# Queries loaded without their zero halves, a block's columns 18 elements apart, the zeros written once on the chip

## The chip, the cores and the metric

The kernel runs on one core of a Trainium2 chip. The metric is the device time of one execution in microseconds; 577.83 us is the median of three runs of the kernel before (577.48 to 578.81). A core has five engines that work side by side, each through its own list of instructions: PE (TensorE, matrix products), DVE (VectorE), ACT (ScalarE), POOL (GpSimd) and SP (SyncE, which here only issues DMA transfers). PE works through pairs of a weight load, which puts one operand into the array, and a matmul, which streams the other operand past it; the profile shows the weight loads as a row of their own, PEld.

## The reference

Two stages run one behind the other, for a batch of 8 sequences of 576 positions and 8 heads of 64. The first is attention with two masks (a window of 32 positions for heads 0 to 3, every fourth position of the last 128 for heads 4 to 7); the second is a mixer that multiplies by cosine and sine of a learned angle, mixes over positions with two matrices, and ends in a channel product with a ReLU.

```python
scores = scale * np.matmul(q, k.transpose(0, 1, 3, 2))
scores = np.where(masks[None, :, :, :], scores, -1000000000.0)
scores = scores - np.max(scores, axis=-1, keepdims=True)
attn = np.exp(scores)
attn = attn / (np.sum(attn, axis=-1, keepdims=True) + 1e-09)
x = np.matmul(attn, v)          # then heads side by side: (8, 576, 512)
theta = x @ w_theta
y = einsum('ts,bsd->btd', w_tok_r, x * cos(theta)) + einsum('ts,bsd->btd', w_tok_i, x * sin(theta))
u = x + y
out = u + np.maximum(u @ w_ch, 0.0)
```

## The kernel before

**Heads in pairs, blocks of 32.** The host reorders the positions of heads 4 to 7 so that both masks become the same band: a block of 32 queries (QB) meets 64 keys (BW). Heads are taken in pairs (NP = 4 pairs for each of the 8 sequences, so 32 pairs in all). A pair stands on 128 partitions, 64 for the depth of each head. One matmul gives the scores of a block for both heads: its weights are 128 x 64, 32 columns for the first head and 32 for the second, and the columns of one head are zero on the 64 partitions of the other. The kernel before gets these zeros from memory: `qT[b, pr]` is 128 x 18 x 64, half of it zeros, 576 KB a pair, and a block's 64 columns lie side by side in it (`q[:, qb]`, L468). The streamed operand is 64 columns of the keys, `k[:, QB*qb : QB*qb + BW]`. The 18 blocks of a pair alternate between the two halves of the output's partitions (`ps[64*e : 64*e+64]`, e = 0 and 1). In fp32 each such product is two weight loads and two matmuls in the profile, so a pair counts 36 of each.

**What follows the scores.** For sequence 0 and four pairs more, the masks are added by PE (L424) and the exponential reads the scores out of PSUM; for the others DVE adds the mask and takes the row maximum (L409) and ACT takes the exponential with its row sum (L504). POOL divides by the sum (L510), DVE turns the blocks (L525), PE multiplies by the values (L617), ACT copies the result out as `x` (L581; for pairs 2 and 3 it writes each element 4 elements, 16 bytes, behind the last, to put the positions back in their order). Then come the angle products (L667 for sequence 0, L685 to L692 for the others), cosine and sine on ACT (L796, L705), their products with `x` on DVE, a split of these into a high and a low part (ACT L644, POOL L646), the token products (L850) and the channel products (L882).

**Weights.** They come as 64-bit integers and are turned into numbers on the chip by `unpack` (DVE L332 and L342, ACT L334 and L340), which reads every second 32-bit word, and split by `split` (ACT L350, POOL L352): first `wth`, then the token weights `wtk`, last the channel weights `wch`.

**What sets the order.** PE's list is pinned everywhere to the order in which the program writes it. For sequence 0, and for the attention of sequence 1 and the start of sequence 2 beside it, a planner (`Order`) sets the order on all engines: each task names an engine and a cost, a DMA's cost is its bytes at a fixed rate (`dma(n)`), and tasks start by rank and by the events that they wait for. So a different cost of a load moves other work. From sequence 1's mixer on (`phase`), the order of PE is written out by tables, and the other engines' order follows from a scheduler.

**The queries' buffers.** `load_qk` takes one of two rotating slots (`take("qk", 2)`), gets a tile `q` of 128 x 18 x 64 from a pool with two buffers, and issues one DMA for q and one for k on SP's queue; after a pair's scores the slot is given back and the load of the pair two further on is issued. `first_loads` does the same for sequence 0 with q in the tiles that later hold `u`. A DMA issue on SP's queue also waits until the transfer eight issues earlier has landed, as the order of instructions shows by the semaphores named there.

Of the kernel before, what the change touches and what calls it, by code (L numbers as in the profile page):

```python
# [8 lines left out]
F32 = mybir.dt.float32  # L9
# [8 lines left out]
B, H, S, D = 8, 8, 576, 64  # L18
DM = H * D
NP = H // 2  # L20
QB = 32
BW = 2 * QB
NJ = S // (2 * QB)
# [38 lines left out]
class Order:  # L62
# [13 lines left out]
    def pin(self, ins):  # L76
        if self.live:
            self.tc.keep_in_program_order(ins)

    def signal(self, event):  # L80
        self.events[event] = self.now
# [49 lines left out]
def dve(n):  # L131
    return 67 + 1.04 * n
# [6 lines left out]
def act(n):  # L139
    return 95 + 0.83 * n  # L140
# [6 lines left out]
def dma(n):  # L147
    return 128 * 4 * n / 360.0
# [3 lines left out]
def build(ctx, tc, qT, kT, vw, wth, wtk, wch, maskb, ident, identb, outT):  # L152
    nc = tc.nc
    cp = ctx.enter_context(tc.tile_pool(name="const", bufs=1))
    ap = ctx.enter_context(tc.tile_pool(name="attn", bufs=2))
# [12 lines left out]
    pin, go, signal = od.pin, od.go, od.signal  # L168

    def pe(ins):  # L170
        tc.keep_in_program_order(ins)
# [27 lines left out]
    def give(tag, n):  # L199
        if od.live:  # L200
            signal(("free", tag, n))
# [11 lines left out]
    def load_qk(n):  # L213
        if n >= B * NP:
            return
        b, pr = divmod(n, NP)
        r = yield from take("qk", 2)
        q = ap.tile([128, 2 * NJ, 2 * QB], F32, tag="q", name=f"q{b}_{pr}")
        k = ap.tile([128, S + 32], F32, tag="k", name=f"k{b}_{pr}")
        yield "DMA", dma(2 * S)  # L220
        pin(nc.sync.dma_start(q, qT[b, pr]))
        yield "DMA", dma(S + 32)
        pin(nc.sync.dma_start(k, kT[b, pr]))
        qks[b, pr] = (q, k, r)
        signal(("qk", b, pr))
# [12 lines left out]
    def load_vb(n):  # L238
# [12 lines left out]
        vs["b", b, pr] = (vb, r)  # L251
        signal(("vb", b, pr))

    KE = S + 32
    first_k = hp.tile([128, 10 * HS], F32R, tag="wt_b", name="first_k").bitcast(F32)
    first_v = hp.tile([128, 8 * HS], F32R, tag="wt_a", name="first_v").bitcast(F32)
# [13 lines left out]
    def first_loads():  # L270
        yield "DMA", dma(3 * BW + 64)
        pin(nc.sync.dma_start(mskb, maskb.bitcast(BF16)))
        pin(nc.sync.dma_start(idb, identb.bitcast(BF16)))
        for pr in range(NP):
            yield from take(f"xh{pr}", 1, 0)
            yield from take(f"u{pr}", 1, 0)
            pqs.append(hp.tile([128, 2, S], F32R, tag=f"xh{pr}", name=f"P0_{pr}").bitcast(F32)[:, 0])
            q = hp.tile([128, 2, S], F32R, tag=f"u{pr}", name=f"q0_{pr}").bitcast(F32)
            q = q.rearrange("p a b -> p (a b)").rearrange("p (a b) -> p a b", b=2 * QB)
            k = first_k[:, KE * pr:KE * pr + KE]  # L280
            yield "DMA", dma(2 * S)
            pin(nc.sync.dma_start(q, qT[0, pr]))
            yield "DMA", dma(KE)
            pin(nc.sync.dma_start(k, kT[0, pr]))
            qks[0, pr] = (q, k, None)
            if pr == 0:
                yield "DMA", dma(128)
                pin(nc.sync.dma_start(idt, ident))
            signal(("qk", 0, pr))
        for pr in range(NP // 2):  # L290
            v = first_v[:, NJ * 128 * pr:NJ * 128 * pr + NJ * 128].rearrange("p (a b) -> p a b", b=128)
            yield "DMA", dma(NJ * 128)
            pin(nc.sync.dma_start(v, vw[0, pr]))
            for h, t in (("a", v[:, :VA]), ("b", v[:, VA:])):
                vs[h, 0, pr] = (t, None)
                signal(("v" + h, 0, pr))
        for pr in range(NP // 2, NP):
            yield from load_va(pr)
            yield from load_vb(pr)

    def consts():
        yield "DVE", 60
        pin(nc.vector.memset(halfpi, math.pi / 2))
        for n in range(2):
            t = cp.tile([128, NJ, 2, 2 * QB], F32, name=f"pt{n}")
            yield "POOL", 1040
            pin(nc.gpsimd.memset(t, 0.0))
            pts.append(t)
        signal("pts")

    def unpack(src, sz, name, stage, early, n, key):

# [102 lines left out]
    def on_pe(b, pr):  # L415
        return b == 0 or (b, pr) in ((1, 2), (1, 3), (2, 0), (2, 1))
# [24 lines left out]
    def scores(b, pr):  # L441
        yield None, ("qk", b, pr)
        if b == 1 and on_pe(b, pr):
            yield None, "sin0"
        if pr >= 1:
            yield None, ("sc", b, pr - 1)
        q, k, rqk = qks[b, pr]
        if b == 0:
            P, rp = pqs[pr].rearrange("p (a b) -> p a b", b=BW), None
        else:  # L450
            rp = yield from take("P", 2)
            P = sp.tile([128, NJ, BW], F32, tag="P", name=f"P{b}_{pr}")
        mx = sp.tile([128, NJ], F32, tag=f"mx{b == 0 and pr}", name=f"mx{b}_{pr}", bufs=1 if b == 0 else 2)
        sm = sp.tile([128, NJ], F32, tag=f"sm{b == 0 and pr}", name=f"sm{b}_{pr}", bufs=1 if b == 0 else 2)
        held = {}
        for g0, g1 in ((0, 5), (5, NJ)):
            ps, rel = yield from bank("s", f"s{b}_{pr}_{g0}")
            ps = ps[:, :(g1 - g0) * BW].rearrange("p (a b) -> p a b", b=BW)
            held[g0] = ps, rel
            masked = on_pe(b, pr)  # L460
            if masked:
                yield "PE", 150
                mask_on_pe(ps, pr, g0, g1)
            yield "PE", 162 * (g1 - g0)
            for n in range(g0, g1):
                for e in range(2):
                    qb = 2 * n + e
                    pe(nc.tensor.matmul(ps[64 * e:64 * e + 64, n - g0], q[:, qb],  # L468
                                        k[:, QB * qb:QB * qb + BW], start=not masked, stop=not masked or n == g1 - 1))
            if masked:  # L470
                go(row_max(b, ps, rel, P, mx, g0, g1, ("mask", b, pr, g0)))
            else:
                go(mask_scores(ps, rel, P, mx, pr, g0, g1, ("mask", b, pr, g0)))
        signal(("sc", b, pr))
        if b == 0:
            give(f"u{pr}", 0)
        else:
            give("qk", rqk)
            go(load_qk(b * NP + pr + 2), RANK["load"])
        if b and on_pe(b, pr):  # L480
            for g0, (ps, rel) in held.items():
                yield None, ("mask", b, pr, g0)
                yield "ACT", 335 * ps.shape[1]
                for n in range(ps.shape[1]):
                    table(nc.scalar.activation(P[:, g0 + n], ps[:, n], AF.Exp, bias=mx[:, g0 + n:g0 + n + 1],
                                               scale=SCALE, accum_out=sm[:, g0 + n:g0 + n + 1]))
                give(*rel)
        else:
            for g0 in (0, 5):
                yield None, ("mask", b, pr, g0)  # L490
        if b == 0:
            yield "ACT", act(S)
            table(nc.scalar.activation(P, P, AF.Exp, scale=SCALE))
            yield "DVE", dve(S)
            pin(nc.vector.tensor_reduce(sm, P, op=ALU.add, axis=mybir.AxisListType.X))
        elif not on_pe(b, pr):
            yield "DVE", 67
            pin(nc.vector.tensor_scalar(mx, mx, -SCALE, None, op0=ALU.mult))  # L498
            if b == 1:
                yield None, "sin0"  # L500
            for n0 in range(0, NJ, 3):
                yield "ACT", 720
                for n in range(n0, n0 + 3):
                    table(nc.scalar.activation(P[:, n], P[:, n], AF.Exp, bias=mx[:, n:n + 1], scale=SCALE,  # L504
                                               accum_out=sm[:, n:n + 1]))
        yield "DVE", 200
        pin(nc.vector.tensor_scalar(sm, sm, 1e-9, None, op0=ALU.add))
        pin(nc.vector.reciprocal(sm, sm))  # L508
        yield "POOL", 1110
        pin(nc.gpsimd.tensor_tensor(P, P, sm.unsqueeze(2).to_broadcast([128, NJ, BW]), op=ALU.mult))  # L510
        probs[b, pr] = P, rp
        signal(("P", b, pr))
# [482 lines left out]
def _arrays(inp):  # L995
    import numpy as np
    q, k, v = inp["q"], inp["k"], inp["v"]
# [5 lines left out]
        return a  # L1003

    q, k, v = perm(q), perm(k), perm(v)
    qT = np.zeros((B, NP, 2, D, 2 * NJ, 2, QB), q.dtype)
    qh = q.reshape(B, NP, 2, 2 * NJ, QB, D).transpose(0, 1, 2, 5, 3, 4)
    for hh in range(2):
        qT[:, :, hh, :, :, hh] = qh[:, :, hh]
    qT = qT.reshape(B, NP, 128, 2 * NJ, 2 * QB)  # L1010
    kT = np.zeros((B, NP, 128, S + 32), k.dtype)
    kT[..., 32:] = k.transpose(0, 1, 3, 2).reshape(B, NP, 128, S)
    vp = np.zeros((B, H, S + 32, D), v.dtype)
# [11 lines left out]
    for n, (j, bound) in enumerate(((1, 0), (0, 0), (2, 144), (4, 288), (6, 432), (7, 432))):  # L1025
        for quad in range(4):
            qb = 2 * j + quad // 2
            p = QB * qb + np.arange(QB)[:, None]
# [30 lines left out]
```

## Time and profile before

| | |
|---|---|
| median of three runs | 577.83 us |
| the profiled execution | 577.82 us |
| its span, first to last instruction | 576.0 us |
| mean granted PE clock | 0.988 |
| queries loaded | 32 DMAs of 576 KB, of 81.02 MB moved on SP's queue |
| score matmuls (L468) | 1152 records, 46.4 us busy |
| ACT busy, POOL busy | 345.2 us, 222.2 us |

Busy time is the sum of the records of an engine; on PE the records of neighbouring matmuls overlap, so what one costs in a run of them is the distance of their starts. In a row of a timeline stand the start, the time taken by the merged run, engine, line, operation, tiles, sizes, the number of instructions (x), and in brackets what the engine waited for. In a table by stretches stand, for each stretch, its length, and for each engine the busy time and in parentheses the number of instructions; then the granted PE clock, the busy share of the DMA engines and GB/s.

### The profile page before, as it was taken

The page shows a single profiled execution, that of the slowest core. Times are in us where ns is not written, and L with a number is a line of the kernel's source. Part 1 is how long each engine was busy: PE and PEld are TensorE (multiplying, and loading weights), DVE is VectorE, ACT ScalarE, POOL GpSimd, SP SyncE. Part 2 cuts the span into 40 slices and gives each one's busy share as a digit, 9 for nine tenths or more (in the row PEclk, how much of TensorE's full clock was granted, in tenths as well). Part 3 has the DMA queues.
Part 4 walks back from the last instruction along what each step waited for, and adds up shares of the span by engine and source line. Part 5 has one row for each costly group of instructions (what it writes and reads, how often), then busy time and mean ns, then how long its engine had stood idle before and what let it go on. Part 6 is the DMA issues. An engine that isn't in the chain of part 4 may idle for free.

```text
span 576.0 us, 13996 instructions
## 1 busy us (share of the span) xinstructions
PE 550.5 (96%) x5464; PEld 501.6 (87%) x5464; DVE 378.0 (66%) x1156; ACT 345.2 (60%) x939; POOL 222.2 (39%) x206
## 2 busy tenths in 40 slices
PE   5997799999999999999999999999999999999997
PEld 4744688879999899988999899988999899989997
DVE  3879798865666668756776768756775767445112
ACT  1498967768555784369555785359556695266110
POOL 2228855525224352226324253226323353325220
PEclk9999699899999999999999999999999999999999
DMA  8991437601747046540746146550747123321002
GB/s 303 400 368 28 165 105 245 216 0 63 231 150 193 32 162 210 169 127 20 268 143 172 64 148 202 181 136 11 252 146 190 69 83 102 77 89 65 18 1 83
DMA packets 45586, 81.91 MB, mean 142 GB/s; under 512 B 3920, under 2 KB 19024, under 8 KB 45520
## 3 DMA queue, kind: packets, MB, share of 16 engines
q1 hardware_dynamic: 45520, 81.02, 43.7%
q8 instruction: 43, 0.70, 0.5%
q14 instruction: 23, 0.19, 0.1%
HBM read 64.49 MB, written 16.52 MB: 141 GB/s over the span
## 4 chain that ended last, share of the span: by engine, by line
DVE 34%; ACT 30%; PE 25%; issue 5%; POOL 2%; DMA 2%; SPq 0%; ACTq 0%; POOLq 0%; DVEq 0%
DVE pt L525 16%; PE y L850 11%; ACT P L504 11%; PE c L882 6%; PE th L685 3%; DVE P L409 3%; ACT K L698 3%; ACT K L787 3%; DVE xh L599 3%; ACT th L796 2%; ACT zh L644 2%; DVE xq L729 2%; DVE K L789 2%; ACT cos L705 2%; ACT x L581 2%
## 5 line engine op out<-in xcount | busy, mean ns | idle before, releaser
L830 POOL TENSOR_TENSOR u<-x,u 128x288 fp32r<-128x288 f32 x64 | 54.7, 858 | 184.6 <-ACT u L828 184.6
L525 DVE STREAM_TRANSPOSE pt<-P 32x288 f32<-32x288 f32 x224 | 105.1, 469 | 12.0 <-POOL P L510 8.9
L882 PE MATMUL c<-u,late_wc 128*128 128x288 f32 x768 | 110.2, 296 | 2.8 <-DVE x L859 2.8
L882 PEld LDWEIGHTS c<-u,late_wc 128*128 128x128 f32 x768 | 106.0, 188 | 6.8 <-DVE x L859 4.0
L850 PE MATMUL y<-wtkh,zh 128*128 128x288 f32 x288 | 90.3, 314 | 1.1 <-ACT zh L644 1.1
L850 PE MATMUL y<-wtkh,zl 128*128 128x288 f32 x288 | 86.2, 299 | 4.0 <-POOL zl L646 4.0
L646 POOL TENSOR_TENSOR zl<-g,zh 128x512 fp32r<-128x512 f32 x40 | 52.3, 1316 | 97.5 <-ACT zh L644 84.5
L504 ACT ACTIVATE P<-P,mx 128x64 f32<-128x64 f32 x216 | 72.0, 335 | 25.8 <-DVE mx L498 25.8
L850 PE MATMUL y<-wtkl,zh 128*128 128x288 f32 x288 | 85.9, 298 | 0.0
L828 ACT CAST u<-x 128x288 fp32r<-128x288 f32 x64 | 26.9, 429 | 86.2 <-DVE x L825 85.5
L685 PE MATMUL th<-wthh,xh 128*128 128x512 f32 x224 | 74.8, 395 | 0.3 <-DVE g L784 0.3
L850 PE MATMUL y<-late_wt_b,zh 128*128 128x288 f32 x320 | 68.1, 297 | 0.0
L825 DVE TENSOR_TENSOR x<-y,x 128x288 f32<-128x288 f32 x64 | 28.1, 448 | 53.6 <-PE y L850 53.5
L850 PEld LDWEIGHTS y<-wtkh,zl 128*128 128x128 f32 x288 | 55.1, 191 | 4.7 <-POOL zl L646 4.7
L850 PEld LDWEIGHTS y<-wtkh,zh 128*128 128x128 f32 x288 | 54.9, 191 | 4.7 <-ACT zh L644 2.3
L850 PE MATMUL y<-late_wt_a,zh 128*128 128x288 f32 x256 | 56.3, 301 | 0.0
L850 PEld LDWEIGHTS y<-wtkl,zh 128*128 128x128 f32 x288 | 55.1, 191 | 0.3 <-issue 0.3
L510 POOL TENSOR_TENSOR P<-P,sm 128x576 f32<-128x576 f32 x32 | 37.5, 1172 | 41.1 <-DVE sm L508 18.1
L850 PEld LDWEIGHTS y<-late_wt_b,zh 128*128 128x128 f32 x320 | 51.4, 189 | 0.3
L685 PEld LDWEIGHTS th<-wthh,xh 128*128 128x128 f32 x224 | 42.0, 188 | 9.2 <-DVE g L784 0.6
L850 PE MATMUL y<-late_wt_b,zl 128*128 128x288 f32 x160 | 47.4, 296 | 0.0
L581 ACT COPY x<-o 128x576 f32<-128x576 f32 x32 | 29.4, 919 | 28.4 <-PE o L617 19.1
(108 smaller groups left out, 1106.3 us busy)
## 6 DMA issues: line engine op xcount, KB each, us to landing
q<-in_qT_dram SPq DMA_DIRECT2D x32, 576.0 KB, 5.2
va<-in_vw_dram SPq DMA_DIRECT2D x30, 320.0 KB, 3.2
k<-in_kT_dram SPq DMA_DIRECT2D x28, 304.0 KB, 5.5
out_dram<-x SPq DMA_DIRECT2D x28, 288.0 KB, 2.4
vb<-in_vw_dram SPq DMA_DIRECT2D x29, 256.0 KB, 3.8
xd<-xq SPq DMA_DIRECT2D x24, 288.0 KB, 5.1
xn<-xd SPq DMA_DIRECT2D x24, 256.0 KB, 3.4
st_wtk<-in_wtk_dram SPq DMA_DIRECT2D x8, 576.0 KB, 8.8
```

The source lines that it names most:

```text
L409: pin(nc.vector.tensor_tensor_reduce(out=P[:, n], in0=ps[:, n - g0], in1=mskb[:, mask_of(pr, n)], op0=ALU.add, op1=ALU.max, scale=1.0, sca ...
L504: table(nc.scalar.activation(P[:, n], P[:, n], AF.Exp, bias=mx[:, n:n + 1], scale=SCALE, accum_out=sm[:, n:n + 1]))
L510: pin(nc.gpsimd.tensor_tensor(P, P, sm.unsqueeze(2).to_broadcast([128, NJ, BW]), op=ALU.mult))
L525: pin(nc.vector.transpose(pmats[b, pr][k0:k0 + QB, :, hh, QB * e:QB * e + QB], P[p0:p0 + QB, :, QB * o:QB * o + QB]))
L581: pin(nc.scalar.copy(dst, src))
L646: pin(nc.gpsimd.tensor_tensor(lo, z, hi.bitcast(F32), op=ALU.subtract))
L685: pe(nc.tensor.matmul(pt, l, r, start=(n == 0), stop=(n == 3 * NC - 1)))
L825: pin(nc.vector.tensor_tensor(x[:, ts], ps, x[:, ts], op=ALU.add))
L828: pin(nc.scalar.copy(uh[b, d][:, ts], x[:, ts]))
L830: pin(nc.gpsimd.tensor_tensor(ul[b, d][:, ts], x[:, ts], uh[b, d][:, ts].bitcast(F32), op=ALU.subtract))
L850: pe(nc.tensor.matmul(ps, l[:, cs], r, start=(n == 0), stop=(n == 3 * NK - 1)))
L882: pe(nc.tensor.matmul(ps, l[:, cs], r[:, ts], start=(n == 0), stop=(n == 3 * NC - 1)))
```

## The change

The host no longer writes zeros: `qT` is 128 x 576 for a pair, with the element of position r of block n at column 18 r + n. On the chip q is 128 x 2 x 576, one half for each head; each head's 64 partitions are loaded into their own half by a DMA of their own, and the other half holds zeros. For the pairs of `load_qk` there are two fixed buffers `qbufs`, whose zeros POOL writes once at the start; for sequence 0's four pairs DVE writes the zeros into the four tiles. A block's weights are now `q[:, :, qb]` of a view whose 64 columns stand 18 elements (72 bytes) apart, through both halves.

```diff
 load_qk:
-        q = ap.tile([128, 2 * NJ, 2 * QB], F32, tag="q", name=f"q{b}_{pr}")
+        q = qbufs[r % 2]
         k = ap.tile([128, S + 32], F32, tag="k", name=f"k{b}_{pr}")
-        yield "DMA", dma(2 * S)
-        pin(nc.sync.dma_start(q, qT[b, pr]))
+        yield "DMA", dma(S)
+        for hh in range(2):
+            rs = slice(64 * hh, 64 * hh + 64)
+            pin(nc.sync.dma_start(q[rs, hh], qT[b, pr, rs]))
...
+    qbufs = [cp.tile([128, 2, S], F32, name=f"q{n}") for n in range(2)]
 first_loads:
             q = hp.tile([128, 2, S], F32R, tag=f"u{pr}", name=f"q0_{pr}").bitcast(F32)
-            q = q.rearrange("p a b -> p (a b)").rearrange("p (a b) -> p a b", b=2 * QB)
+            for hh in range(2):
+                pin(nc.vector.memset(q[64 * hh:64 * hh + 64, 1 - hh], 0.0))
...
-            yield "DMA", dma(2 * S)
-            pin(nc.sync.dma_start(q, qT[0, pr]))
+            yield "DMA", dma(S)
+            for hh in range(2):
+                rs = slice(64 * hh, 64 * hh + 64)
+                pin(nc.sync.dma_start(q[rs, hh], qT[0, pr, rs]))
 consts, behind the two memsets of pt:
+        for q in qbufs:
+            for hh in range(2):
+                yield "POOL", 580
+                pin(nc.gpsimd.memset(q[64 * hh:64 * hh + 64, 1 - hh], 0.0))
 scores:
+        q = q.rearrange("p h (r n) -> p (h r) n", n=2 * NJ)
...
-                    pe(nc.tensor.matmul(ps[64 * e:64 * e + 64, n - g0], q[:, qb],
+                    pe(nc.tensor.matmul(ps[64 * e:64 * e + 64, n - g0], q[:, :, qb],
                                         k[:, QB * qb:QB * qb + BW], start=not masked, stop=not masked or n == g1 - 1))
 _arrays:
-    qT = np.zeros((B, NP, 2, D, 2 * NJ, 2, QB), q.dtype)
...
+    qT = q.reshape(B, H, 2 * NJ, QB, D).transpose(0, 1, 4, 3, 2).reshape(B, NP, 128, S)
```

Line numbers of the changed kernel are some ten higher. SP's list begins like this before (mskb and idb are the mask and an identity, `first_k` and `q_0` to `q_3` are sequence 0's keys and queries):

```order
L272 DMA mskb<-in_maskb_dram 128x384
L273 DMA idb<-in_identb_dram 128x128
L282 DMA q_0_105<-in_qT_dram 128x1152
L284 DMA first_k<-in_kT_dram 128x608
L288 DMA idt<-in_ident_dram 128x128
L282 DMA q_1_115<-in_qT_dram 128x1152
```

and like this in the changed kernel:

```order
L279 DMA mskb<-in_maskb_dram 128x384
L280 DMA idb<-in_identb_dram 128x128
L292 DMA q_0_106<-in_qT_dram 64x576 x2
L294 DMA first_k<-in_kT_dram 128x608
L298 DMA idt<-in_ident_dram 128x128
L292 DMA q_1_119<-in_qT_dram 64x576 x2
```

Each load of queries is two issues of half the partitions, so the first keys are the fifth issue instead of the fourth.

Some forty issues later on SP, where sequence 2's queries and the four channel weights (`st_wch`) are loaded, the list before is:

```order
L221 DMA q_1_1072<-in_qT_dram 128x1152
L325 DMA st_wch_1063<-in_wch_dram 128x1024
L325 DMA st_wch_1113<-in_wch_dram 128x1024
L223 DMA k_1_1073<-in_kT_dram 128x608
L234 DMA va_3_1110<-in_vw_dram 128x640
L250 DMA vb_2_1111<-in_vw_dram 128x512
L221 DMA q_2_1228<-in_qT_dram 128x1152
L325 DMA st_wch_1233<-in_wch_dram 128x1024
L325 DMA st_wch_1262<-in_wch_dram 128x1024
```

and in the changed kernel:

```order
L339 DMA st_wch_1050<-in_wch_dram 128x1024
L223 DMA q_91<-in_qT_dram 64x576 x2
L225 DMA k_1_1088<-in_kT_dram 128x608
L236 DMA va_3_1126<-in_vw_dram 128x640
L339 DMA st_wch_1129<-in_wch_dram 128x1024
L252 DMA vb_2_1127<-in_vw_dram 128x512
L223 DMA q_90<-in_qT_dram 64x576 x2
L339 DMA st_wch_1227<-in_wch_dram 128x1024
L225 DMA k_2_1237<-in_kT_dram 128x608
L339 DMA st_wch_1273<-in_wch_dram 128x1024
```

The first two channel weights are now issued one ahead of `q_91` and one behind `va_3`, where both stood behind `q_1`.

DVE's list in the changed kernel begins with the zeros, where before only `halfpi` stood ahead of the first row maximum (`mx_0`):

```order
L287 MEMSET q_0_106 64x576 x2
L313 MEMSET halfpi 128x1
L287 MEMSET q_1_119 64x576 x2
L287 MEMSET q_2_130 64x576 x2
L287 MEMSET q_3_153 64x576 x2
L444 TENSOR_REDUCE mx_0_122<-s_0_0_124 128x5
```

Eight writes of 64 x 576 were put ahead of DVE's first work; on POOL four of the same size stand behind the two memsets of `pt`. From sequence 1's mixer on, PE's order is the same in both kernels; on SP the keys of each sequence's fourth pair, which stood ahead of the four stores of the turned `x` (`xd`), now stand behind them.

More of the change, by code (lines that the diff above doesn't have):

```diff
@@ L1005, in _arrays @@
     q, k, v = perm(q), perm(k), perm(v)
-    qT = np.zeros((B, NP, 2, D, 2 * NJ, 2, QB), q.dtype)
[L1007 to L1010, printed above, removed]
+    qT = q.reshape(B, H, 2 * NJ, QB, D).transpose(0, 1, 4, 3, 2).reshape(B, NP, 128, S)
     kT = np.zeros((B, NP, 128, S + 32), k.dtype)
```

## The prediction

> **What bounds the kernel now.** I begin with the head of the page.
>
> ```profile
> span 576.0 us, 13996 instructions
> ...
> PE 550.5 (96%) x5464; PEld 501.6 (87%) x5464; DVE 378.0 (66%) x1156; ACT 345.2 (60%) x939; POOL 222.2 (39%) x206
> ```
>
> PE is busy 96% of the span; no other engine comes near. A mean over stages can hide a stage with another bound, so the second view is the table by stretches.
>
> ```profile
> 0.00:24.00 24.00, 16.20 (x312) 13.58 (x312) 11.85 (x31) 6.10 (x10) 5.71 (x9) 1.00 0.92 343
> 24.00:72.00 48.00, 40.69 (x324) 25.31 (x324) 40.74 (x103) 42.46 (x98) 28.60 (x22) 0.89 0.57 207
> 72.00:128.00 56.00, 51.65 (x562) 45.98 (x561) 47.24 (x103) 39.85 (x122) 27.61 (x24) 0.97 0.43 146
> 128.00:192.00 64.00, 64.00 (x655) 60.12 (x654) 42.18 (x152) 37.16 (x114) 23.03 (x22) 1.00 0.50 150
> ...
> 454.00:520.00 66.00, 65.42 (x601) 60.99 (x600) 39.71 (x110) 42.51 (x97) 26.01 (x24) 1.00 0.26 77
> ```
>
> The columns are length, PE, PEld, DVE, ACT, POOL, PE clock, DMA share, GB/s. From 128 us on PE is full: whatever PE does longer there, the kernel ends later by as much. The third view, what PE waited for behind 128 us, says that no transfer is among it:
>
> ```profile
> PE c L882 <- DVE x L859: 2.8, 5, 0.6
> ```
>
> Before 128 us PE (92.34 of 104 us from 24 to 128), DVE and ACT share the bound, and only in the first 24 us is DMA nearly always busy (0.92). So halving the queries' bytes can pay at the start alone, while a dearer score product would be paid nearly everywhere. How many of these there are in each stretch:
>
> ```profile
> 0.00:24.00 24.00, 8.88 (x144) 7.53 (x144) 1.00 0.92 343
> 24.00:72.00 48.00, 3.88 (x72) 3.37 (x72) 0.89 0.57 207
> 72.00:128.00 56.00, 6.48 (x144) 5.33 (x144) 0.97 0.43 146
> 128.00:192.00 64.00, 4.93 (x144) 4.54 (x144) 1.00 0.50 150
> ...
> 454.00:520.00 66.00, 2.49 (x72) 2.27 (x72) 1.00 0.26 77
> ```
>
> These are L468 alone: 144 + 216 before 128 us, and behind it five stretches of 144 and one of 72, which is 792; 1152 in all.
>
> **The weight load with a stride.** This is the step that I hold for decisive. A score matmul keeps its streamed operand (keys, side by side); its weights are now 64 columns 72 bytes apart. What a load costs today:
>
> ```profile
> L468 PEld LDWEIGHTS s<-k,q x1008: 132/138/232, 42.9 to 476.0; 128*64 128x64 f32 x168
> ...
> 143.01 1.13 PEld L468 LDWEIGHTS s<-k,q 128*64 128x64 f32 x36 [0.16 <-issue]
> ...
> L685 PEld LDWEIGHTS th<-wthl,xh 128*128 128x128 f32 x112 | 21.0, 188 | 3.7
> ...
> L689 PEld LDWEIGHTS th<-wthl,xh 128*64 128x64 f32 x21 | 2.8, 134 | 1.3
> ```
>
> 36 loads take 1.13 us, one of them 0.138, so they start (1.13 - 0.138)/35 = 28.3 ns apart. 64 columns more cost 188 - 134 = 54 ns, 0.84 ns a column: 64 columns are 54 ns of reading. That fits a distance of 28.3 ns only if two loads run side by side, as the blocks' alternation between the two halves of the output lets them, and then there are 2.6 ns of slack in 56.6. If a column takes longer to read, I expect the distance to grow with it.
>
> No PE instruction of this trace reads with a stride, so the price must be bounded. The nearest rows are ACT's, with the same number of elements side by side, at 16 bytes and at 8:
>
> ```profile
> 149.31 0.64 ACT L581 COPY x<-o 128x576 f32<-128x576 f32 x1 [0.28 <-PE o L617]
> ...
> 161.31 1.20 ACT L581 COPY x<-o 128x576 f32<-128x576 f32 x1
> ...
> 60.04 0.72 ACT L334 ACTIVATE st_wtk<-st_wtk 128x576 f32<-128x576 f32 x1
> ```
>
> The second copy is a pair whose `x` is written 16 bytes apart: 1.20 against 0.64 us, 1.88 times, 0.97 ns more for each element. The third reads and writes every second word, 8 bytes apart, and pays next to nothing. So on this chip an SBUF access whose elements lie 16 bytes or more apart runs at about half speed, for one engine and for writes. The low end for PE is nothing; below nothing I exclude, since no element gets nearer to the next. The high end is ACT's 0.97 ns for 64 columns, 62 ns a load, with no overlap. I take ACT's ratio on today's distance, 28.3 x 1.88 = 53.1 ns, **24.8 ns more** for each load, because it is nearest to the one row that shows a stride of this kind.
>
> [...]
>
> **The sum of this term.** Behind 128 us: 792 x 24.8 ns = 19.6 us, all on the path. From 24 to 128 us: 216 x 24.8 = 5.4 us, of which I count half, 2.7, since PE has 11.66 us of idle time there and DVE and ACT are busy for 88 and 82 of the 104 us. In the first 24 us PE is slow anyway:
>
> ```profile
> 7.00 1.18 PEld L468 LDWEIGHTS s<-first_k,q 128*64 128x64 f32 x20 [3.91 <-DMA q<-in_qT_dram]
> ...
> L468 PEld LDWEIGHTS s<-first_k,q x144: 132/227/232, 7.0 to 22.2; 128*64 128x64 f32 x144
> ```
>
> (1.18 - 0.227)/19 = 50 ns, only 3 short of 53: 144 x 3 = 0.4 us. Together **+22.7 us**. With the high end it would be 1008 x 62 ns + 144 x 40 ns = +68 us.
>
> **The loads.** 288 KB fewer lie ahead of the first keys, for which PE waits:
>
> ```profile
> 7.03 1.34 PE L468 MATMUL s<-first_k,q 128*64 128x64 f32 x20 [3.62 <-DMA first_k<-in_kT_dram]
> ...
> 1.64 0.42 SPq L282 DMA_DIRECT2D q<-in_qT_dram  x1
> 2.11 0.43 SPq L284 DMA_DIRECT2D first_k<-in_kT_dram  x1
> ...
> GB/s 0 118 286 373 294 351 392 418 418 433 401 400 386 409 410 404 390 390 392 397 393 401 406 395 397 390 394 340 111 31 5 0 0 0 0 0 0 78 320 269
> ```
>
> The last row cuts the first 60 us into 40 slices; around 5 us it moves some 330 GB/s, so 288 KB are 0.9 us. The keys' issue comes one place later, 0.47 us. I take **-0.6 us** (0 to -0.9). After that PE, DVE and ACT hand work to each other and no row waits for a query. The 28 later loads save bytes that nobody waits for; their 28 extra issues of 0.3 to 0.4 us fall on a queue that mostly waits.
>
> [...]
>
> **The zeros.** The nearest rows for a write of 64 x 576, and what waits behind it:
>
> ```profile
> 0.73 2.05 POOL L307 MEMSET pt<- 128x1152 f32 x2 [0.29 <-POOLq L1045]
> ...
> 24.16 0.75 DVE L495 TENSOR_REDUCE sm<-P 128x9 f32<-128x576 f32 x1
> ...
> 8.40 0.49 DVE L430 TENSOR_REDUCE mx<-s 128x5 f32<-128x320 f32 x1 [7.54 <-PE s L468]
> ...
> POOL P L510 <- DVE sm L508: 18.1, 5, 10.9
> ```
>
> DVE: eight of at most 0.75 us are 6.0, from 0.8 to 6.8 us, inside the 7.54 us in which DVE waits for the first scores. PE's first score matmul now also waits for the first two, done by 2.3 us, ahead of its keys; all of PE is queued behind it. POOL: half a `pt` each, 4 x 0.51 = 2.1 us, inside its wait of 10.9. Both cost 0; without the cover they would cost at most 6.0 and 2.1 us. The pool's two buffers become two fixed ones: the same two slots, given back at the same place.
>
> **The order.** With cheaper loads the planner puts other work forward before 128 us, on all engines. Two rows bound what that can give: a wait for channel weights in the chain of waits, and PE's idle time around it.
>
> ```profile
> 99.62 5.64 DMA st_wch<-in_wch_dram
> ...
> 100.00:104.00 4.00, 2.49 (x27) 2.10 (x27) 3.82 (x10) 3.04 (x20) 1.07 (x1) 0.74 0.84 268
> ```
>
> PE idles 1.51 us there. A better place of the first two `st_wch` can win that, a worse one of anything else lose as much again; I take 0, and 1.5 to 2.5 us to either side. Behind 128 us PE's order is the same. There the fourth pair's keys go behind the `xd` stores, some 8 us later on SP:
>
> ```profile
> 236.49 0.42 SPq L223 DMA_DIRECT2D k<-in_kT_dram  x1
> 240.81 3.78 SPq L736 DMA_DIRECT2D xd<-xq  x4
> ...
> L468 PEld LDWEIGHTS s<-k,q x216: 132/138/139, 208.2 to 280.4; 128*64 128x64 f32 x108
> ```
>
> After 236 us the next scores run at about 280: 35 us of cover, cost 0.
>
> The sum on the profiled execution's 577.82 us (1.8 us outside its span; the median is 577.83): 577.82 + 22.7 - 0.6 = **599.9 us**.
>
> **The rivals.** *A: the stride is free.* Then 577.2 us, 574.5 to 579.5 with the order's share: not slower. [...] It decides as long as a strided load of 64 columns takes no more than two distances, 56.6 ns. Against it: today's 54 ns leave 2.6 ns to that point. [...] *B: the stride is free and the order wins*: with 1.5 us from the `st_wch` wait, 575.7 us. For it: PE's idle time is all before 128 us. Against: DVE and ACT are busy for most of it. *C: the strided loads don't overlap*: 577.82 + 68 - 0.6 = 645 us, if one path reads for both halves of the array; the distance of 28.3 ns speaks against. [...]
>
> **How the numbers follow.** Forecast 0.56; its own range is 589 (15 ns a load, 792 x 15 = 11.9 us) to 611 (31 ns a load, two side by side at ACT's 0.97 ns a column, all of it on the path: 1008 x 31 = 31.2, and 1.3 at the start). A 0.22, B 0.16, C 0.06. A change within 0.2%, 1.16 us, is about what a measurement of this kernel can't tell from none: of A 0.13 is the same, 0.05 slower, 0.04 faster. So faster 0.20, same 0.13, slower 0.67. The range from 574.5 to 611 leaves out C, some 0.05 above the forecast's own end, and 0.04 below B.
>
> **What would show it.** The distance of L468's loads in a run of 36, behind 128 us: about 53 ns and a run of 1.9 us in place of 1.13 if the forecast holds, 28 if A does, 90 with C. The rest of PE's rows must keep their times. The first score matmul should start near 6.4 us; a wait of L468 for DVE or POOL would show the zeros uncovered, one for q the halves late. The forecast is wrong if the loads' distance keeps its 28 ns.

## The result, and the profile after

The changed kernel takes 599.35 us (median of six runs, 597.93 to 601.01) against 577.75 us of the kernel before in the same job (six runs, 576.67 to 579.83). The ratio is 1.0372, with a 95% interval from 1.0346 to 1.0397. It is 21.6 us slower; the forecast was 599.9 us.

The page of the changed kernel's profile begins so (span, busy time by engine, and further down SP's queue and the chain of work that ended last, by engine):

```profile
span 599.2 us, 14040 instructions
...
PE 578.0 (96%) x5464; PEld 530.0 (88%) x5464; DVE 386.7 (65%) x1164; ACT 347.6 (58%) x939; POOL 224.5 (37%) x210
...
q1 hardware_dynamic: 46032, 71.58, 39.2%
...
PE 87%; DVE 5%; POOL 2%; DMA 2%; ACT 2%; issue 1%; SPq 1%; DVEq 0%; POOLq 0%
...
L483 PE MATMUL s<-k,q 128*64 128x64 f32 x1008 | 65.2, 283 | 0.2 <-DVE K L804 0.2
L483 PEld LDWEIGHTS s<-k,q 128*64 128x64 f32 x1008 | 61.3, 210 | 4.1 <-issue 2.9
```

PE is again busy for 96% of the span, but for 27.5 us more (578.0 against 550.5) with as many matmuls, 5464. The transfers shrank as meant, from 81.02 to 71.58 MB on SP's queue, and did not buy time. The chain that ended last now lies on PE for 87%; the kernel before had long pieces of it on DVE and ACT:

```profile
DVE 34%; ACT 30%; PE 25%; issue 5%; POOL 2%; DMA 2%; SPq 0%; ACTq 0%; POOLq 0%; DVEq 0%
```

Where the time came from shows in the timeline of the score products (L483). First the run that answers to the 36 loads of before at 143.01 us, then the first loads and matmuls of the program:

```profile
147.56 2.16 PEld L483 LDWEIGHTS s<-k,q 128*64 128x64 f32 x36 [0.17 <-issue]
...
6.09 1.26 PEld L483 LDWEIGHTS s<-first_k,q 128*64 128x64 f32 x20 [2.75 <-issue]
6.12 1.41 PE L483 MATMUL s<-first_k,q 128*64 128x64 f32 x20 [2.46 <-DMA first_k<-in_kT_dram]
```

The view of line L483 gives the duration of one load (least, median, most, in ns), then the first and last start:

```profile
L483 PEld LDWEIGHTS s<-k,q x1008: 188/211/221, 43.1 to 499.1; 128*64 128x64 f32 x168
...
L483 PEld LDWEIGHTS s<-first_k,q x144: 188/210/221, 6.1 to 22.3; 128*64 128x64 f32 x144
```

The 36 loads take 2.16 us in place of 1.13, so their starts lie (2.16 - 0.211)/35 = 55.7 ns apart, 27.4 more than before. One load lasts 211 ns in place of 138. The stretches show the same price: all lines first, L483 alone below.

```profile
0.00:24.00 24.00, 17.57 (x322) 15.23 (x324) 16.36 (x40) 6.58 (x11) 7.95 (x13) 0.93 0.89 295
24.00:72.00 48.00, 41.76 (x320) 25.71 (x315) 42.40 (x99) 43.62 (x99) 29.93 (x21) 0.93 0.57 182
72.00:128.00 56.00, 51.42 (x539) 46.16 (x537) 45.83 (x103) 35.76 (x115) 25.06 (x23) 0.97 0.40 125
128.00:192.00 64.00, 63.33 (x630) 60.21 (x631) 40.00 (x148) 37.73 (x114) 23.86 (x23) 1.00 0.41 116
```

```profile
0.00:24.00 24.00, 10.28 (x144) 9.01 (x144) 0.93 0.89 295
24.00:72.00 48.00, 5.08 (x72) 4.49 (x72) 0.93 0.57 182
72.00:128.00 56.00, 10.14 (x144) 9.00 (x144) 0.97 0.40 125
128.00:192.00 64.00, 9.05 (x144) 8.66 (x144) 1.00 0.41 116
```

From 128 to 192 us PE is full before (64.00 of 64 us) and nearly full now (63.33). The 144 score matmuls there are busy for 9.05 us where before it was 4.93, 4.12 more, and 25 other matmuls found no room (630 against 655). The channel products (L897), the largest group, kept their 188 ns a load.

The two runs of 36 also cut the difference in two: it was 147.56 - 143.01 = 4.55 us when they began, and from there to the end the kernels take 451.64 and 432.99 us, 18.65 more. The changed kernel's profiled execution, 601.01 us, is the longest of its six and 1.66 us above their median; the kernels with the same stride below take 451.67 and 451.68 us behind the run, so that excess lies in the 4.55.

### The profile page after: what moved, and what is told of

It reads as the page before. It is cut to its first block, busy times and chain, and to the rows that moved or that the text cites. A ratio compares the mean times of both kernels' runs of the same rounds, so it can differ in the third digit from the quotient of the medians.

```text
span 599.2 us, 14040 instructions
## 1 busy us (share of the span) xinstructions
PE 578.0 (96%) x5464; PEld 530.0 (88%) x5464; DVE 386.7 (65%) x1164; ACT 347.6 (58%) x939; POOL 224.5 (37%) x210
## 2 busy tenths in 40 slices
DMA packets 46098, 72.48 MB, mean 121 GB/s; under 512 B 4432, under 2 KB 19536, under 8 KB 46032
## 3 DMA queue, kind: packets, MB, share of 16 engines
q1 hardware_dynamic: 46032, 71.58, 39.2%
## 4 chain that ended last, share of the span: by engine, by line
PE 87%; DVE 5%; POOL 2%; DMA 2%; ACT 2%; issue 1%; SPq 1%; DVEq 0%; POOLq 0%
PE y L865 38%; PE c L897 16%; PE th L700 12%; PE s L483 10%; PE o L632 6%; POOL zl L661 1%; DVE pt L540 1%; PE th L705 1%; DMA st_wch<-in_wch_dram 1%; PE pT L576 1%; PE th L704 1%; DMA first_k<-in_kT_dram 1%; PE th L682 1%; DVE g L765 1%; DVE st_wtk L356 1%
## 5 line engine op out<-in xcount | busy, mean ns | idle before, releaser
L897 PE MATMUL c<-u,late_wc 128*128 128x288 f32 x768 | 108.9, 295 | 0.0
L897 PEld LDWEIGHTS c<-u,late_wc 128*128 128x128 f32 x768 | 105.9, 188 | 2.8
L483 PE MATMUL s<-k,q 128*64 128x64 f32 x1008 | 65.2, 283 | 0.2 <-DVE K L804 0.2
L483 PEld LDWEIGHTS s<-k,q 128*64 128x64 f32 x1008 | 61.3, 210 | 4.1 <-issue 2.9
L525 POOL TENSOR_TENSOR P<-P,sm 128x576 f32<-128x576 f32 x32 | 38.8, 1212 | 47.7 <-ACT xh L608 16.1
```

Of the source, the lines that this page charges most:

```text
L483: pe(nc.tensor.matmul(ps[64 * e:64 * e + 64, n - g0], q[:, :, qb], k[:, QB * qb:QB * qb + BW], start=not masked, stop=not masked or n == g ...
L897: pe(nc.tensor.matmul(ps, l[:, cs], r[:, ts], start=(n == 0), stop=(n == 3 * NC - 1)))
```

## The experiments

My theory was that the distance of the weight columns, and it alone, makes the kernel slower: 16 bytes of SBUF (a line, below) that hold only one column cost PE the time of two, as ACT's copy with its elements written 16 bytes apart took 1.20 us in place of 0.64. The rivals were that the halved loads, their zeros or the moved order cost the time, or that PE's price has another law (it grows with the distance, or with any distance at all). In each job the kernel before ran beside; its medians there were 577.80 us (first four runs), 578.32 (next four) and 578.29 (last three).

### The change without its stride

The halves, the zeros on the chip and the new order stay, but the loads put each block's 32 columns of a head side by side, in runs of 128 bytes, and the zeros between them. Against the changed kernel:

```diff
+    def runs(q, hh):
+        return q.rearrange("p h s -> p (h s)").rearrange("p (n h r) -> p n h r", h=2, r=QB)[:, :, hh]
...
-            pin(nc.sync.dma_start(q[rs, hh], qT[b, pr, rs]))
+            pin(nc.sync.dma_start(runs(q, hh)[rs], qT[b, pr, rs].rearrange("p (n r) -> p n r", r=QB)))
...
-        q = q.rearrange("p h (r n) -> p (h r) n", n=2 * NJ)
+        q = q.rearrange("p h s -> p (h s)").rearrange("p (n c) -> p n c", c=2 * QB)
...
-    qT = q.reshape(B, H, 2 * NJ, QB, D).transpose(0, 1, 4, 3, 2).reshape(B, NP, 128, S)
+    qT = q.transpose(0, 1, 3, 2).reshape(B, NP, 128, S)
```

> The changed kernel with one thing taken back: q's halves are still loaded apart and the zeros still written on the chip, but a block's 64 columns lie side by side again (each DMA writes runs of 32 elements, 128 bytes). The order on PE, DVE and ACT is that of the changed kernel. Theory 'the stride is the cost': a run of 36 weight loads takes 1.13 us again (28.3 ns apart, record 138 ns), and the time is within 3 us of the kernel before, 575 to 580 us. Rival 'halves, zeros or the new order are the cost': loads at 28 ns as well, but the time stays near 599 us. In between (585 to 592) would say that the planner's order costs part of it.

Measured: 580.68 us (578.6 to 583.17), ratio 1.0056 (1.0035 to 1.0078). In the timeline the run of 36 is that of before again:

```profile
143.74 1.13 PEld L487 LDWEIGHTS s<-k,q 128*64 128x64 f32 x36 [0.17 <-issue]
```

Taking the stride away thus takes 18.7 us off the 599.35. What is left, +0.6%, is small but clear of no change: everything else in the change together costs time.

### The stride alone

The kernel before, with its zeros from memory, its one load a pair and its order; only the host stores the columns of all 18 blocks interleaved, and a block's weights are read 72 bytes apart. Against the kernel before:

```diff
+WIDTHS = (18,)
+    def qcols(q, qb):
+        g0 = 0
+        for w in WIDTHS:
+            if qb < g0 + w:
+                break
+            g0 += w
+        flat = q[:, g0:g0 + w].rearrange("p a b -> p (a b)").rearrange("p (c w) -> p c w", w=w)
+        return flat[:, :, qb - g0]
...
-                    pe(nc.tensor.matmul(ps[64 * e:64 * e + 64, n - g0], q[:, qb],
+                    pe(nc.tensor.matmul(ps[64 * e:64 * e + 64, n - g0], qcols(q, qb),
```

> The kernel before with one thing added: the zeros still come from memory in one transfer of 576 KB and every engine's order is that of before, but the host lays the columns of a block 18 elements (72 bytes) apart. Theory 'the stride is the cost': runs of 36 loads take 2.16 us (56 ns apart), 597 to 602 us. Rival: 577 to 579 us.

Measured: 598.88 us (598.6 to 599.25), ratio 1.0363 (1.0338 to 1.0388). The run of 36 loads:

```profile
145.53 2.17 PEld L478 LDWEIGHTS s<-k,q 128*64 128x64 f32 x36 [0.16 <-issue]
```

One view of the weights, without any other part of the change, makes the kernel slower by 3.6%. Both directions agree on the cause: the stride is enough for the loss, and without it nearly all of the loss is gone. They don't add up to one number: alone it costs 21.1 us, taken away it gives back 18.7. So the rest of the change costs 2.9 us without the stride, and with it 0.5 us (599.35 against 598.88), which these runs can't tell from nothing.

### How the price goes with the distance

The same kernel, with the blocks interleaved by 2, 4 or 3 in place of 18, so that a block's columns lie 8, 16 or 12 bytes apart:

```diff
-WIDTHS = (18,)
+WIDTHS = (2, 2, 2, 2, 2, 2, 2, 2, 2)
...
-WIDTHS = (18,)
+WIDTHS = (4, 4, 4, 4, 2)
...
-WIDTHS = (18,)
+WIDTHS = (3, 3, 3, 3, 3, 3)
```

> As e2, with the columns of two blocks interleaved: 2 elements, 8 bytes apart, two columns in each 16 bytes. Theory 'a line of 16 bytes must be hit twice', as ACT's rows show it: nothing lost, 28 ns, 577 to 579 us. Rival 'any stride but one element costs': near 56 ns and 598 us, or part of it.

> As e2, with 16 of the 18 blocks interleaved by fours, 4 elements, 16 bytes apart, one column in each 16 bytes; the last two blocks at 8 bytes. Theory 'a line of 16 bytes must be hit twice': 56 ns for 16 blocks of 18, so about 16/18 of e2's loss, 594 to 600 us. Rival 'the price grows with the distance (72 bytes)': loads between 28 and 50 ns, below 592 us.

> As e2 (zeros from memory, order of before), with the blocks interleaved by threes: 3 elements, 12 bytes apart, so 16 columns fall into 12 lines of 16 bytes, 4 of them hit twice and 8 once. Theory 'each line costs what two side-by-side columns cost': a load needs 48 lines of 1.75 ns in place of 64 columns, about 42 ns apart, a run of 36 of 1.65 us, 587 to 590 us. Rival 'a threshold at 16 bytes between columns': 28 ns, 577 to 579 us.

Measured: 8 bytes 578.44 us (575.68 to 579.86), ratio 1.0007 (0.999 to 1.0025); 16 bytes 597.73 us (596.8 to 598.39), 1.0342 (1.0315 to 1.0368); 12 bytes 585.94 us (585.0 to 587.47), 1.0139 (1.0117 to 1.016). The same run of 36 in the timelines of the three, in this order:

```profile
144.35 1.17 PEld L478 LDWEIGHTS s<-k,q 128*64 128x64 f32 x36 [0.16 <-issue]
```

```profile
145.82 2.12 PEld L478 LDWEIGHTS s<-k,q 128*64 128x64 f32 x36 [0.16 <-issue]
```

```profile
144.81 1.68 PEld L478 LDWEIGHTS s<-k,q 128*64 128x64 f32 x36 [0.16 <-issue]
```

Taking off one load (0.138, 0.217 and 0.176 us, the medians) and dividing by 35 gives the distances of the starts. A line is an aligned 16 bytes, and the second column counts how many of them 64 columns touch. In the 16-byte kernel 4 of the 36 loads lie at 8 bytes, so its 54.4 ns is a mean over both; the row gives an estimate for the 32 others, (35 x 54.4 - 4 x 29.5)/31.

| bytes between columns | lines | ns between loads | ns a line | change of the time, us |
|---|---|---|---|---|
| 4 (before) | 16 | 28.3 | | |
| 8 | 32 | 29.5 | 0.92 | +0.6 |
| 12 | 48 | 43.0 | 0.90 | +7.6 |
| 16 (16 blocks of 18) | 64 | 57.6 | 0.90 | +19.9 |
| 72 | 64 | 55.7 | 0.87 | +21.1 |

In these five kernels the price follows the lines, about 0.9 ns each, with a floor of 28 to 30 ns for up to 32 of them. A distance of 8 bytes costs nothing that shows (29.5 ns, ratio 1.0007), 12 bytes cost half (14.7 ns a load, against 27.4 at 72 bytes), and from 16 to 72 bytes nothing is added (57.6 and 55.7 ns). With two columns in a line PE's loads kept their distance here, and with one it about doubled. The 12-byte kernel's median came out some 1 us below the expected range, though its loads have about the distance that was forecast; its profiled execution, the longest of the four at 587.47 us, lies inside. No run settles that microsecond; in that profile PE's wait of 2.8 us for DVE behind 128 us (L882 in the prediction) is gone, as in the other kernels that pay for a stride, which takes 2.8 us off a price of only 11.6 there (792 x 14.7 ns).

### Keys with a distance instead of queries

The weights lie side by side as before; the other operand, the 64 keys that stream past them, is stored 76 bytes apart. Against the kernel before:

```diff
+    def kcols(k, qb):
+        return k.rearrange("p (r m) -> p m r", m=2 * NJ + 1)[:, qb:qb + 2]
...
-                                         k[:, QB * qb:QB * qb + BW], start=not masked, stop=not masked or n == g1 - 1))
+                                         kcols(k, qb), start=not masked, stop=not masked or n == g1 - 1))
```

> The kernel before, weights side by side, but the streamed operand with a stride: the keys laid so that a block's 64 columns are two rows of 32, 19 elements (76 bytes) apart. Theory 'each SBUF read of PE pays below two hits a line': matmuls of a run 56 ns apart, 597 to 601 us. Rival 'only the weight load pays': 28 ns, 577 to 579 us.

Measured: 603.52 us (602.19 to 605.75), ratio 1.0444 (1.0421 to 1.0467), more than expected. In the timeline of PE the second run of 36 matmuls (the first, at 145.82 us, takes 2.48 us) is:

```profile
153.11 2.44 PE L471 MATMUL s<-k,q 128*64 128x64 f32 x36
```

and in the view of line L471 a matmul's duration (least, median, most, in ns):

```profile
L471 PE MATMUL s<-k,q x1008: 282/310/366, 43.4 to 501.6; 128*64 128x64 f32 x168
```

The starts lie (2.44 - 0.31)/35 = 60.9 ns apart. So the price isn't a matter of the weight load alone: what PE streams pays as well, and in this run 5 ns more than weights 72 bytes apart. The keys also lie in two rows of 32, which the weights don't; no run separates that from the 5 ns.

### The rest of the change: which part loses 0.6%?

The first experiment left +0.6% where the prediction had -0.6 us. Five kernels look for it. The first is the changed kernel with the planner told the old size of the loads, so that PE and ACT get the order of before. The second takes halves and zeros in that old order, with columns 8 bytes apart, which cost nothing that showed above (ratio 1.0007). The third takes from the change nothing but two issues, each with half of the partitions, still with the zeros from memory and in the old order. The fourth takes the new order alone: the kernel before, and the planner told the costs of the change. The fifth splits each load of the kernel before in two as well, but by columns, so that each part fills all 128 partitions.

```diff
 first, against the changed kernel (both places):
-        yield "DMA", dma(S)
+        yield "DMA", dma(2 * S)
 second, against the changed kernel (and dma(2 * S) as above):
+        return q.rearrange("p h s -> p (h s)").rearrange("p (g h c) -> p g h c", h=2, c=BW)[:, :, hh]
...
+        q = q.rearrange("p h s -> p (h s)").rearrange("p (g c w) -> p g c w", c=2 * QB, w=2)
...
-                    pe(nc.tensor.matmul(ps[64 * e:64 * e + 64, n - g0], q[:, :, qb],
+                    pe(nc.tensor.matmul(ps[64 * e:64 * e + 64, n - g0], q[:, qb // 2, :, qb % 2],
 third, against the kernel before (both places):
-        pin(nc.sync.dma_start(q, qT[b, pr]))
+        for hh in range(2):
+            rs = slice(64 * hh, 64 * hh + 64)
+            pin(nc.sync.dma_start(q[rs], qT[b, pr, rs]))
 fourth, against the kernel before:
-        yield "DMA", dma(2 * S)
+        yield "DMA", dma(S)
...
+        for _ in range(4):
+            yield "POOL", 580
 fifth, against the kernel before (both places):
-        pin(nc.sync.dma_start(q, qT[b, pr]))
+        for hh in range(2):
+            bs = slice(NJ * hh, NJ * hh + NJ)
+            pin(nc.sync.dma_start(q[:, bs], qT[b, pr, :, bs]))
```

> The changed kernel (stride 72 bytes, halves, zeros on the chip) with the planner told the old cost of a load of queries, so that PE's and ACT's order is that of before, and DVE's and POOL's but for the zeros. Theory 'the new order costs some 2 us ahead of the first fourth-pair scores of the b=2 stage': 596.5 to 598.5 us, below the changed kernel's 599.35 and e2's 598.88 by what the earlier first keys give, some 0.5 to 0.9. Rival 'halves or zeros cost it': 599 to 601 us.

> Halves and zeros on the chip as in the changed kernel, the order of before as in e7, and columns 8 bytes apart (blocks interleaved by twos, each DMA writes runs of 64 elements, 256 bytes). No stride cost by e3. If the loads' saving is real, 576.5 to 577.5 us, at best 0.2% below before; if short runs or halves eat it, 578 to 580 us.

> The kernel before (zeros from memory, no stride, order of before) with one thing changed: each load of queries is two DMAs of 64 partitions. No fewer bytes, no zeros written. Theory 'the loss of e7 and e8 comes from two DMAs of 64 partitions in place of one of 128': each takes SP about 0.56 us to issue as in the changed kernel, against 0.33 to 0.43 for a whole one, the channel weights behind them are issued later, and the time is 579.5 to 582 us, as e8. Rival 'the zeros cost it' (DVE and POOL writes at the start): 577 to 578.5 us.

> The kernel before with the planner told the cost of half a load (and of POOL's four zeros), so that PE's and ACT's order is that of the changed kernel, but q still comes whole, with zeros and without a stride. Theory 'the order wins the 2 us by which the changed kernel lies below e7': 575 to 576.5 us. Rival 'the order only makes good what the halves cost': 577 to 579 us.

> As e10, but the two DMAs split the columns, 9 blocks each on all 128 partitions. If the loss hangs on 64 partitions, issues take 0.33 to 0.43 us each and the time is 577 to 579 us; if it hangs on there being two DMAs, on the queue and on the eight transfers that may be under way, it is near e10's.

Measured, as ratios to the kernel before:

| kernel | us | ratio | interval |
|---|---|---|---|
| change, old order | 601.41 | 1.0399 | 1.038 to 1.0417 |
| halves and zeros, 8 bytes, old order | 581.38 | 1.0059 | 1.004 to 1.0077 |
| two issues of 64 partitions, nothing saved | 583.06 | 1.0074 | 1.0048 to 1.01 |
| new order alone | 580.22 | 1.0032 | 1.0016 to 1.0048 |
| two issues of 128 partitions, nothing saved | 579.16 | 1.0016 | 0.9995 to 1.0036 |

All five medians lie above the ranges named for them, by 0.2 to 1.4 us, and three of the runs went against me. The old order did not make the changed kernel better, the halves did not save their 0.6 us, and the new order alone is no gain of 2 us but a loss of 0.3%. All these losses lie ahead of the run of 36, which starts at 143 to 148 us: from its start to the end the first experiment's kernel and the second to fifth of these take 432.9 to 433.1 us, the kernel before 432.99. The first of the five takes 451.68 us there, the stride alone 451.67.

Halved loads without a costly stride were run only with short pieces: 32 columns (128 bytes) a piece in the first experiment and 64 (256 bytes) in the second of the five, 115730 and 78866 DMA packets in the pages against 46098 in the changed kernel. A part of their 0.6% may be the price of the pieces; no run shows that. Two runs with long pieces speak for the halves nevertheless: the third, also with 46098 packets, and the first, which at the same order and stride lies above the stride alone (1.0399 against 1.0363, the intervals just meet).

What tells most is the pair of the third and the fifth, which differ only in how a load is cut. Their first 24 us in the table by stretches, the third's first and the fifth's below (the last two columns are the busy share of the DMA engines and GB/s):

```profile
0.00:24.00 24.00, 15.47 (x260) 12.85 (x260) 9.73 (x25) 4.76 (x7) 4.57 (x8) 1.00 0.92 272
```

```profile
0.00:24.00 24.00, 15.41 (x348) 13.13 (x348) 13.41 (x34) 7.48 (x13) 5.71 (x9) 1.00 0.92 345
```

The pages' rows of DMA issues, in the same order (number of issues, KB each, median us from issue to landing):

```profile
q<-in_qT_dram SPq DMA_DIRECT2D x64, 288.0 KB, 5.1
```

```profile
q<-in_qT_dram SPq DMA_DIRECT2D x64, 288.0 KB, 4.2
```

The pages' rows of SP's queue (packets, MB, and the time that the packets took, as a share of the time of 16 engines):

```profile
q1 hardware_dynamic: 46032, 81.02, 48.9%
```

```profile
q1 hardware_dynamic: 50128, 81.02, 44.1%
```

And the issues of one load in their timelines of SP:

```profile
220.88 1.11 SPq L223 DMA_DIRECT2D q<-in_qT_dram  x2
```

```profile
215.53 0.81 SPq L223 DMA_DIRECT2D q<-in_qT_dram  x2
```

At the same busy share, 0.92, transfers to 64 partitions each bring the whole to 272 GB/s, those to 128 partitions to 345 (before: 343), and over the whole span the same 81.02 MB keep the DMA engines busy for 48.9% in place of 44.1% (before: 43.7%). With the former, 260 matmuls are done after 24 us, with the latter 348. But before it is 312 with the same rate as the latter, and 312 again in the second kernel, with 273 GB/s: I put that spread down mostly to the single profile, in which PE's loads stay slow for longer or less long (in those 24 us 260 loads take 12.85 us in the third's, 49 ns each, and 348 take 13.13 us in the fifth's, 38 ns each). Each issue also takes SP 0.55 us in place of 0.40; so do the keys' issues behind them, though they fill 128 partitions (0.59 in place of 0.43 us at the start, as in the changed kernel), so the time isn't that of the halves alone. Here the second transfer, to the other half of the partitions, did not bring the rate back: 272 against 345 GB/s. The halved loads of the change carry half the bytes; with them the core moves 295 GB/s in its first 24 us, at a share of 0.89.

A second place where the halves may lose is in the first kernel of the five. It stands level with the stride alone until the score products at 95 us (95.46 and 95.18 us), and begins the run of 36 at 148.22 us where the stride alone has 145.53. Between 98 and 110 us lie the queries of sequence 2 and the channel weights. SP's issues, the changed kernel in the old order first, and the stride alone below it:

```profile
99.08 1.13 SPq L223 DMA_DIRECT2D q<-in_qT_dram  x2
101.15 2.96 SPq L339 DMA_DIRECT2D st_wch<-in_wch_dram  x2
```

```profile
98.80 0.33 SPq L222 DMA_DIRECT2D q<-in_qT_dram  x1
101.10 1.61 SPq L326 DMA_DIRECT2D st_wch<-in_wch_dram  x2
```

The two halves take 1.13 us to issue in place of 0.33, and the channel weights behind them are issued within 2.96 in place of 1.61 us. PE's longest wait around there is 2.6 us for ACT's exponential, and 1.1 us with the stride alone:

```profile
PE s L438 <- ACT P L500: 2.6, 1, 2.6
```

```profile
PE s L434 <- ACT P L495: 1.1, 1, 1.1
```

That these two waits differ because of SP's issues is not shown, and other profiles speak against it: the channel weights take 2.96 us to issue also with whole loads and columns 8 bytes apart, and 2.94 with loads cut by columns, and neither kernel is clearly slower than before. The wait itself, in the old order, is 2.6 to 3.8 us with halves of the partitions and 1.0 to 2.4 us with whole loads, but 3.3 us with loads cut by columns. Which wait takes up the loss by the halves stays open.

## Why the prediction was right

The direction, the place and the mechanism were right, and the sum came within 0.6 us. Two of its terms were off, and the errors cancelled in part, so a part of that closeness is luck.

**The stride, +22.7 us.** Right as the step that decides, and confirmed by the two runs that add and remove it. The distance was taken from ACT's ratio as 53.1 ns; it is 55.7, so the term of 24.8 ns a load should have been 27.4, and behind 128 us 792 x 27.4 = 21.7 us in place of 19.6. The kernels differ by 18.65 us there, not 21.7, because the step "all on the path" was too strict: before, PE idled 2.8 us for DVE's `x` behind 128 us, and in the changed kernel that row is gone. The longer PE needs, the more often DVE is done in time: 21.7 - 2.8 = 18.9. The row is gone in all six profiles whose loads or keys pay for a stride, and stands with 1.6 to 2.8 us in the seven others. Ahead of the run of 36 the stride alone costs 145.53 - 143.01 = 2.52 us, and 2.7 + 0.4 was forecast with half of the loads hidden. (The upper end of the range, 611, adds up to 610.3: 577.82 + 31.2 + 1.3.)

**The first 24 us** were priced at the 50 ns a load that the loads took there before. The 20 loads take 1.26 us where before it was 1.18, (1.26 - 0.210)/19 = 55 ns: the stride's distance holds there too, and it isn't added to the 50 ns.

**The loads, -0.6 us.** This step failed. Its first half held: the first score product starts at 6.12 us, 0.91 earlier than before, and DVE's first row maximum at 7.58 in place of 8.40. But it was not kept. Halves without a costly stride are 0.6% slower (the second of the five), and two half loads that save nothing 0.7% (the third). What failed is that the later loads were priced at nothing, as bytes that nobody waits for and extra issues that "fall on a queue that mostly waits". The extra issues alone, with loads cut by columns, cost 0.16%, which can't be told from nothing; cut by partitions the loads are slower each at one busy share (272 against 345 GB/s), and that was in no term. In the changed kernel itself, under the stride, the rest of the change costs the 0.5 us named above. The 0.91 us by which the first scores came earlier are small beside what the loads lost as a whole: the kernel of the second experiment of the five stands 581.38 - 578.32 = 3.1 us above its reference.

**The zeros, 0.** Right. DVE wrote its eight in 0.54 us each, and POOL its four in 2.40 us (2.1 forecast), both ahead of their first work. The timeline of the changed kernel:

```profile
0.93 0.54 DVE L287 MEMSET q<- 64x576 f32 x1 [0.93 <-PEq L1056]
...
2.73 2.40 POOL L323 MEMSET q<- 64x576 f32 x4
...
5.86 0.54 DVE L287 MEMSET q<- 64x576 f32 x1 [0.16 <-issue]
...
7.58 0.49 DVE L444 TENSOR_REDUCE mx<-s 128x5 f32<-128x320 f32 x1 [1.18 <-PE s L483]
```

DVE's last zeros are done at 6.40 us, and then it still waits 1.18 us for PE's scores. No row has L483 waiting for DVE or POOL at the start. The kernel with two issues but no zeros on the chip loses as much as the one with them, so they aren't hidden somewhere else either.

**The order, 0 with 1.5 to 2.5 us to either side.** Alone it costs +0.32% (0.16% to 0.48%), 1.9 us: inside these bounds. The hope for the wait for `st_wch` (rival B) fell. Yet the changed kernel in the new order is not slower than in the old one (1.0372 against 1.0399, the intervals meet). So the order's effect isn't a number that adds to the others; which waits take it up with halves and not without them stays open.

**The rivals.** A and B fell with the distance of 55.7 ns. A's chance of 0.22 was my estimate, with no strided row of PE to go by; 64 columns took 28.3, 43.0 and 55.7 ns, by where they lay, so the number of columns alone did not set a load's time in these runs. C, loads that no longer overlap, fell as well: its distance was to be 90 ns.

Together: 18.65 us behind the run of 36 (19.6 forecast) and 4.55 ahead of it (2.5 forecast), 23.2 us between the two profiled spans. By the medians it is 21.6 us, and since the part behind the run hardly differs from profile to profile, some 2.95 us are left ahead of it. The waits that PE no longer has came off the first number; what the first keys gained is not to be found in the second.

## What to carry to other kernels

Both operands of these fp32 matmuls paid for a distance in SBUF: weights 16 and 72 bytes apart brought the starts of their loads from 28.3 to 57.6 and 55.7 ns, keys 76 bytes apart those of the matmuls to 60.9 ns. Weights 8 bytes apart stayed at 29.5 ns and cost nothing that showed (ratio 1.0007), so a host that interleaves weights like these should interleave by two. Before halving a transfer, look for a row in which someone waits for it, and count the issues and the partitions of what replaces it: loads cut by partitions lost 0.6% here even with half the bytes, loads cut by columns at most 0.4%. Where PE is full, a change in the distance of its starts, times the number of loads, is the forecast, less the idle time that the longer PE work will fill (here 21.7 - 2.8 = 18.9 us, and 18.65 measured).

## What the runs showed of the hardware

- Weight columns cost by the aligned 16 bytes, the lines, that they touched: 64 fp32 columns took 28 to 30 ns for up to 32 lines, 43.0 for 48, and 55.7 (72 bytes apart) and 57.6 (16 bytes apart, estimated above) for 64. The prediction had expected half speed from 16 bytes on; that 12 bytes fall between was expected, at 42 ns, only when they were run.
- The streamed operand paid too, in the one run for it more than the weights: 60.9 ns with keys 76 bytes apart, against 55.7 with weights 72 bytes apart.
- In the program's first score products the stride shows little: 20 loads start 55 ns apart with it and 50 ns apart before, against 55.7 and 28.3 later. A load's median is 210 ns in the first 24 us and 211 later, where before it was 227 and 138. How long the loads stay slow differs between profiles: in the first 24 us 312 loads take 13.58 us before, 44 ns each, and with loads cut by columns 348 take 13.13 us, 38 ns each.
- With loads cut into two halves of the partitions the core moves 272 GB/s in the first 24 us at a DMA share of 0.92, with loads cut by columns 345 GB/s at the same share; over the span the same bytes take 48.9 and 44.1% of the DMA engines' time.
